# Chunk 0's early work of a fused scan and gated layer in another order

## The chip, the cores and the metric

The kernel runs on one core of one Trainium2 chip. The metric is the device time of one execution in microseconds (us). The core has a matrix engine (TensorE, PE in the profile; its weight loads are PEld), a vector engine (VectorE, DVE), a scalar engine (ScalarE, ACT), a general engine (GpSimd, POOL) and an engine that only issues transfers (SyncE, SP). Each engine works through its own queue in order and waits for the others with semaphores. Transfers between the main memory and the core (DMA) are issued on the queue of SP or ACT.

## The reference

Two parts, the second fed by the first. The first part is a scan over a sequence in chunks, for 4 batches, 8 heads, 768 positions, head size 32 and state size 16:

```python
L = exp(cum[:, :, :, None] - cum[:, :, None, :]) * causal      # decay from j to i
CB = einsum('bhin,bhjn->bhij', Cc, Bc)
y_intra = einsum('bhij,bhjd->bhid', CB * L, xc)
y_inter = einsum('bhin,bhnd->bhid', Cc, state) * exp(cum)[:, :, :, None]
y = y_intra + y_inter
state = decay_full * state + einsum('bhjn,bhjd->bhnd', Bc * decay_from_j, xc)
```

The second part takes y as 3072 rows of 256 numbers: h = x @ w_in (256 x 2048), g = h * cos(h), and out = g @ w_out (2048 x 256).

## The kernel before

The 768 positions are cut into six chunks of 128. Chunks 0 and 1 are cut once more, into four units of 64 positions (0 and 1 are chunk 0), so that the first rows of the second part can start early; the two halves of the partitions (index s) hold two pairs of batches. The order on every engine is written out by hand: instructions stand on an engine's queue in the order of the Python calls, and the framework only adds the semaphores.

Once y of a unit is there, `first` multiplies it by w_in, `wind` and `gate` take the cosine on ACT and DVE, `gated` multiplies, and `second` multiplies by w_out. From about 35 us on these steps alternate on PE without a pause until the end, with the later chunks' scan work in between. The weights come as pieces of 512 KB ("in" 0 to 7, "out" 0 to 7), and `grade` and `join` (L252 to L289) turn each into fp32 on ACT, POOL and DVE.

Units 0 and 1, the part that is changed, go like this:

- The transfers (L291 to L306). ACT's queue issues four loads of C. SP's queue issues a (L213), two halves of B for unit 0 (L294), the first piece of w_in, two halves of x for unit 0 (L297), the first half of B for unit 1 (L298), the second piece of w_in, two halves of x for unit 1, the first piece of w_out, and so on. The second half of B for unit 1 is issued on ACT's queue (L314), after ACT has loaded its table and taken one sine.
- The decays. `share_a` (L346) multiplies the clipped a by a mask of heads: DVE for heads 0 to 5 in one instruction, POOL for heads 6 and 7. `spread_a` (L383) is a matmul that copies these rows to all partitions, into a PSUM bank; the bank's tag ("h", "o" or the pair of "scan") says which buffers it shares. `decays0` (L391) is a scan on DVE from that bank into `lam`. With n=2 each covers half of the heads, 256 columns.
- The turns. Four quarters of C are brought into the order of `c0`, two by POOL (L365) and two by ACT (L366). `turn_c` (L414) transposes them on PE into one bank `tp`. `take_c` (L424) copies unit k's part of this bank twice, each scaled by a mask (column t of `slot`), into `cuts[k]`; both copies run on ACT. `turn_b` (L429) transposes B into another bank on PE, and its return value copies it to `turned` on ACT.
- The product. `inner` (L472) multiplies turned B and `cuts` on PE into the banks g; `weights` (L483) multiplies g by `lam` on DVE; `finish0` (L491) forms y on PE: L504 with the state, L513 for the new state, L521 for the unit itself. `weigh0` (L402) prepares the operand `sc` of L513 on POOL.
- `fill` (L81) are two matmuls on the matrix of ones (L78), ahead of everything else on PE; their results aren't used.

The order of the calls for unit 0 stands in L887 to L915, that for unit 1 in L916 to L923 and in `first_steps` (L1011).

Of the kernel before, what the change touches and what calls it, by code (L numbers as in the profile page):

```python
# [8 lines left out]
FP32 = mybir.dt.float32  # L9
# [3 lines left out]
ALU = mybir.AluOpType  # L13
# [12 lines left out]
def kernel(  # L26
# [12 lines left out]
    nc = tc.nc  # L39
    V, ACT, G, PE = nc.vector, nc.scalar, nc.gpsimd, nc.tensor  # L40
# [3 lines left out]
    P = 128  # L44
# [5 lines left out]
    HH = H // 2  # L50
# [18 lines left out]
    def bank(shape, name, tag):  # L69
        return psum.tile(shape, FP32, tag=tag, bufs=2, name=name)  # L70
# [7 lines left out]
    ones = const.tile([P, P], FP32, name="ones")  # L78
    V.memset(ones, 1.0)

    def fill(dst, times=1):  # L81

        for _ in range(times):
            PE.matmul(dst, lhsT=ones, rhs=ones.unsqueeze(1).to_broadcast([P, dst.shape[1], P]),
                      start=True, stop=True, skip_group_check=True)


    a_all = dram.tile([NB, H, S], FP32, name="a_all")
# [30 lines left out]
    c4 = both[0][:, 1].rearrange("p (h r) n -> p h r n", h=H)  # L119
    xrs = {}  # L120

    def load_b(k, s, eng=nc.sync, of=B):

        eng.dma_start(out=(bs if of is B else cs)[k][s * W:(s + 1) * W].rearrange(
                          "p q (h n) -> p (q h) n", h=H),
                      in_=of[2 * s:2 * s + 2, :, k * W:(k + 1) * W, :]
                      .rearrange("b h i n -> i (b h) n"))
# [7 lines left out]
    def load_x(k, s, eng=nc.sync):  # L135
        if k not in xrs:
            t = loads.tile([P, 2, 2, H, D], FP32, tag="xr", name="xr")
            xrs.update({k // 2 * 2 + i: t[:, i] for i in range(2)})
        eng.dma_start(out=xrs[k][s * W:(s + 1) * W].rearrange("p q h d -> p (q h) d"),
                      in_=x[2 * s:2 * s + 2, :, k * W:(k + 1) * W, :]  # L140
                      .rearrange("b h i d -> i (b h) d"))
# [55 lines left out]
    def load_along(c, seqs=range(NB)):  # L197
# [5 lines left out]
        for b in seqs:  # L203
            for q in range(4 if b % 2 else 1):
# [9 lines left out]
                      in_=a[:, :, 0:P].rearrange("b h (k i) -> (b h) k i", k=2))  # L214
# [15 lines left out]
    def kept(which, i):  # L230
        return (w_in[:, :, i * WC:(i + 1) * WC] if which == "in" else
                w_out[:, i * WF:(i + 1) * WF])

    def fetch(which, i, eng=nc.sync):
        src = (moe_w_in[:, i * WC:(i + 1) * WC].rearrange("(k p) f -> p k f", p=P)
               if which == "in" else
               moe_w_out[i * WF * P:(i + 1) * WF * P, :].rearrange("(f p) m -> p f m", p=P))
        if src.dtype == FP32:
            eng.dma_start(out=kept(which, i), in_=src)
            return  # L240
        words[which, i] = t = conv.tile([P, 2 * WC, 2], U32, tag="words", bufs=8, name="words")
        eng.dma_start(
            out=t.rearrange("p (k f) w -> p k (f w)", k=src.shape[1]), in_=src.bitcast(U32))
# [30 lines left out]
    def join(which, i):  # L274


        parts = held.pop((which, i), ())
        for e, (high, bits, last) in enumerate(parts):
            V.tensor_scalar(out=bits, in0=bits, scalar1=3, scalar2=0x3FFFFFFF,  # L279
                            op0=ALU.logical_shift_left, op1=ALU.bitwise_and)  # L280
            V.scalar_tensor_tensor(out=bits, in0=high, scalar=0xC0000000, in1=bits,  # L281
                                   op0=ALU.bitwise_and, op1=ALU.bitwise_or)
            dst = kept(which, i)
            if len(parts) > 1:
                dst = dst[:, :, e * P:(e + 1) * P]
            else:
                bits, last = (ap.rearrange("p (k f) -> p k f", k=dst.shape[1])
                              for ap in (bits, last))
            G.tensor_tensor(out=dst.bitcast(U32), in0=bits, in1=last, op=ALU.add)  # L289
# [5 lines left out]
    fetch("in", 0)  # L295
    for s in range(2):
        load_x(0, s)  # L297
    load_b(1, 0)  # L298
    fetch("in", 1)
    for s in range(2):  # L300
        load_x(1, s)
# [2 lines left out]
        out=a_in, in_=a.rearrange("(u b) h (c p) -> (b h c) u p", u=NU, p=P))  # L304
# [6 lines left out]
    quarter = const.tile([P, 1], FP32, name="quarter")  # L311
    V.memset(quarter, HALF_PI)
    ACT.activation(const.tile([P, 1], FP32, name="sine"), quarter, AF.Sin)
    load_b(1, 1, nc.scalar)  # L314
    V.memset(a0z[:, :, 0:1], 0.0)
    for r in (slice(NB * H, W), slice(W, P)):
        V.memset(a0z[r, :, 1:], 0.0)
# [28 lines left out]
    def share_a(k, eng, h0, h1):  # L346
        eng.tensor_tensor(out=a0s[k][:, h0:h1],
                          in0=a0z[:, k:k + 1].to_broadcast([P, h1 - h0, W]),
                          in1=mine[:, h0:h1].unsqueeze(2).to_broadcast([P, h1 - h0, W]),
                          op=ALU.mult)  # L350

    share_a(0, G, 6, H)
    share_a(0, V, 0, 6)
    whose_of(1)
    G.memset(along1[:, :, 0:1], 0.0)
    G.tensor_scalar(out=a0[:, 1], in0=a0[:, 1], **clip)
    for p in range(2):
# [4 lines left out]
                  in_=mine.unsqueeze(2).to_broadcast([P, H, N]))  # L362
    c0 = loads.tile([P, 2, 2, 4, 2, N], FP32, tag="blocks", name="c0").rearrange(
        "p a b c d n -> p (a b c d n)").rearrange("p (r h n) -> p r h n", r=4, h=H)
    G.tensor_copy(out=c0[:, 0:2].rearrange("p r h n -> p h r n"), in_=c4[:, :, 0:2])  # L365
    ACT.copy(out=c0[:, 2:4].rearrange("p r h n -> p h r n"), in_=c4[:, :, 2:4])  # L366
    G.memset(lead, 0.0)
    G.memset(lead[:, :, 0:1], 1.0)
    slot = const.tile([P, 2], FP32, name="slot")
# [10 lines left out]
    lams, scs, turns0, cuts, gs, m_of, rTs, states0 = {}, {}, {}, {}, {}, {}, {}, {}  # L380
    spread = {}

    def spread_a(k, p, i=0, n=1, tag="o"):  # L383

        ps = (pair("a_ps")[:, 0] if tag is None else bank([P, 4 * P], "a_ps", tag))
        ps = spread[k, p, i] = ps[:, 0:H * W // n].rearrange("p (h i) -> p h i", i=W)
        PE.matmul(ps, lhsT=whose[:, p].rearrange("p s i -> p (s i)"),
                  rhs=a0s[k][:, i * H // n:(i + 1) * H // n], start=True, stop=True,
                  skip_group_check=True)

    def decays0(k, p, i=0, n=1):  # L391

        if p == i == 0:
            lams[k] = scan.tile([P, 2, H, W], FP32, tag="lam", bufs=4, name="lam")
        flat = "p h i -> p (h i)"
        hs = slice(i * H // n, (i + 1) * H // n)
        rows_ = spread.pop((k, p, i)) if k < 2 else arows[k][:, p]
        V.tensor_tensor_scan(out=lams[k][:, p, hs].rearrange(flat), data0=rows_.rearrange(flat),
                             data1=unit0[:, hs].rearrange(flat), initial=0.0,
                             op0=ALU.mult, op1=ALU.add)  # L400
# [13 lines left out]
    def turn_c():  # L414

        tp = bank([P, 4, P], "tp", "o")
        for r in range(4):
            PE.transpose(tp[:, r], c0[:, r].rearrange("p h n -> p (h n)"), ident)
        tp = tp.rearrange("p r (b k g) -> p k b g r", b=NB, k=2)

        def of(k, dst, **v):
            ACT.activation(dst.rearrange("p b (g r) -> p b g r", r=4), tp[:, k], AF.Copy, **v)

        def take(k):  # L424
            for t in range(2):
                of(k, cuts[k][:, t].rearrange("p q (s i) -> p (q s) i", s=2), scale=slot[:, t:t + 1])
        return take, of

    def turn_b(k, tp):  # L429

        for p in range(2):
            PE.transpose(tp[:, 2 * k + p], bs[k][:, p], ident)
        return lambda: ACT.copy(out=bTs[k], in_=tp[:, 2 * k:2 * k + 2])
# [38 lines left out]
    def inner(k, t):  # L472

        gs[k, t] = g = pair("g")
        bT, cT = bTs[k], cuts[k]
        for p, s, q in ((p, s, q) for p in range(2) for s in range(2) for q in range(2)):
            ss, q_ = slice(s * W, (s + 1) * W), 2 * t + q
            r = slice(32 * q_, 32 * q_ + 32)
            PE.matmul(g[ss, q, p * P:(p + 1) * P].rearrange("p (t i) -> p t i", t=2),  # L479
                      lhsT=bT[r, p, ss], rhs=cT[r, :, p, ss], start=True, stop=True,  # L480
                      tile_position=(32 * q_, s * W), skip_group_check=True)
# [221 lines left out]
    hp, turns, gT, o = {}, {}, {}, {}  # L703
# [180 lines left out]
                              in_=ob[s * W:(s + 1) * W].rearrange("p h m -> p (h m)"))  # L884


    fill(bank([P, 4, P], "warm", "o"), 1)  # L887
    fill(bank([P, 2, P], "warm", "o"), 1)
    spread_a(0, 0, 0, 2, None)
    spread_a(0, 0, 1, 2, None)  # L890
    spread_a(0, 1, 0, 2, "h")
    for p, i in ((0, 0), (0, 1), (1, 0)):
        decays0(0, p, i, 2)
    spread_a(0, 1, 1, 2, "h")
    decays0(0, 1, 1, 2)
    spread_a(1, 0, 0, 2, None)
    decays0(1, 0, 0, 2)
    take_c, of_c = turn_c()
    tp_b = bank([P, 4, P], "tp", "o")
    take_b = turn_b(0, tp_b)  # L900
    spread_a(1, 0, 1, 2, "h")
    decays0(1, 0, 1, 2)
    take_c(0)
    take_b()
    weigh0(0)
    grade("in", 0)
    for t in range(2):
        inner(0, t)
    spread_a(1, 1, tag="h")
    for q in range(2):  # L910
        weights(0, q)
    take_c(1)
    join("in", 0)
    decays0(1, 1)
    take_s0, _ = finish0(0)  # L915
    take_b = turn_b(1, tp_b)  # L916
# [262 lines left out]
```

## Time and profile before

| | |
|---|---|
| time, median of 3 runs | 369.6 us (369.3 to 369.76) |
| the profiled execution's own time | 369.82 us |
| its span in the profile | 368.0 us |
| PE busy | 361.3 us (98%) |
| DVE busy | 276.2 us (75%) |
| ACT busy | 173.0 us (47%) |
| POOL busy | 217.6 us (59%) |

The span is measured between the first and the last instruction of the program; 1.8 us of the execution's own time lie around it. Busy shares are means over the whole span; the stretch that the change touches is its first 18 us, and there they are different. In the first 36 us, by the table of busy time in each stretch, PE is busy for 33.3 us, DVE for 30.1, ACT for 23.0 and POOL for 22.9, and from about 3 to 28 us the 16 DMA engines are busy nearly without a gap.

In the lines of the timeline, the two first numbers are the start of a group of instructions and its time, then come the engine, the source line, the operation, the tile written and the tiles read, and in brackets how long the engine was idle before and what ended that. A queue of an engine (SPq, ACTq) issues transfers. In the chain, the number after a tile is the source line.

### The profile page before, as it was taken

The page shows a single profiled execution, that of the slowest core. Times are in us where ns is not written, and L with a number is a line of the kernel's source. Part 1 is how long each engine was busy: PE and PEld are TensorE (multiplying, and loading weights), DVE is VectorE, ACT ScalarE, POOL GpSimd, SP SyncE. Part 2 cuts the span into 40 slices and gives each one's busy share as a digit, 9 for nine tenths or more (in the row PEclk, how much of TensorE's full clock was granted, in tenths as well). Part 3 has the DMA queues.
Part 4 walks back from the last instruction along what each step waited for, and adds up shares of the span by engine and source line. Part 5 has one row for each costly group of instructions (what it writes and reads, how often), then busy time and mean ns, then how long its engine had stood idle before and what let it go on. Part 6 is the DMA issues. An engine that isn't in the chain of part 4 may idle for free.

```text
span 368.0 us, 8760 instructions
## 1 busy us (share of the span) xinstructions
PE 361.3 (98%) x3390; PEld 325.4 (88%) x3390; DVE 276.2 (75%) x451; ACT 173.0 (47%) x300; POOL 217.6 (59%) x340
## 2 busy tenths in 40 slices
PE   8999999999999999999999999999999999999995
PEld 5688888889999899999999999899999989999995
DVE  7789998578699858978867987777887783544463
ACT  3597757454445345354344444434444534444442
POOL 6567747579786558765446674544584444554441
PEclk9999999999999999999999999999999999999999
DMA  9995948457226746731055341020100010010011
GB/s 139 239 373 141 186 112 134 56 146 190 73 77 89 137 111 90 215 94 32 6 78 115 93 130 45 0 53 2 24 18 2 0 30 2 2 29 2 0 30 30
DMA packets 97706, 30.57 MB, mean 83 GB/s; under 512 B 71456, under 2 KB 93568, under 8 KB 97664
## 3 DMA queue, kind: packets, MB, share of 16 engines
q1 hardware_dynamic: 95376, 29.55, 35.4%
q10 hardware_dynamic: 2288, 0.46, 0.8%
q8 instruction: 27, 0.44, 0.5%
q14 instruction: 15, 0.12, 0.1%
HBM read 26.58 MB, written 3.34 MB: 81 GB/s over the span
## 4 chain that ended last, share of the span: by engine, by line
PE 91%; DVE 3%; DMA 2%; ACT 2%; issue 1%; SPq 1%; ACTq 0%
PE hp L724 44%; PE o L833 34%; PE o L795 6%; DMA xr<-in_x_dram 2%; PE y L674 2%; PE g L622 2%; DVE mag L279 1%; PE y L654 1%; PE y L521 1%; DVE mag L281 1%; PE g L479 1%; PE y L504 1%; DVE w L737 1%; PE o L878 1%; ACT mag L266 0%
## 5 line engine op out<-in xcount | busy, mean ns | idle before, releaser
L724 PE MATMUL hp<-yT,w_in 128*128 128x256 f32 x768 | 183.2, 382 | 0.3 <-DVE gT L751 0.3
L724 PEld LDWEIGHTS hp<-yT,w_in 128*128 128x128 f32 x768 | 139.3, 190 | 19.9 <-issue 3.2
L776 POOL TENSOR_TENSOR gd<-gT 128x256 f32<-128x256 f32 x79 | 60.0, 760 | 96.7 <-DVE gT L751 84.6
L746 ACT ACTIVATE w<-w,quarter 128x512 f32<-128x512 f32 x96 | 69.2, 721 | 84.4 <-DVE w L737 84.3
L737 DVE SCALAR_TENSOR_TENSOR w<-hp,k 128x512 f32<-128x512 f32 x96 | 65.8, 686 | 43.2 <-ACT k L731 43.0
L731 ACT ACTIVATE k<-hp 128x512 int32<-128x512 f32 x96 | 57.1, 594 | 78.9 <-PE hp L724 78.5
L751 DVE TENSOR_TENSOR gT<-hp,w 128x512 f32<-128x512 f32 x96 | 65.3, 680 | 33.2 <-ACT w L746 21.7
L833 PE MATMUL o<-words,gd 128*128 128x128 f32 x474 | 65.9, 275 | 0.0
L833 PEld LDWEIGHTS o<-words,gd 128*128 128x128 f32 x474 | 59.3, 192 | 0.0
L833 PEld LDWEIGHTS o<-w_out,gT 128*128 128x128 f32 x316 | 47.5, 191 | 4.0
L779 POOL TENSOR_TENSOR gd<-gT,gd 128x128 f32<-128x128 f32 x79 | 46.0, 582 | 6.2
L833 PE MATMUL o<-w_out,gT 128*128 128x128 f32 x316 | 48.0, 274 | 0.0
L778 POOL TENSOR_TENSOR gd<-gT,gd 128x128 f32<-128x128 f32 x79 | 44.0, 556 | 6.2
L581 DVE TENSOR_TENSOR_SCAN lam<-arow,unit 128x512 f32<-128x512 f32 x32 | 42.0, 1314 | 0.0
L833 PE MATMUL o<-words,gT 128*128 128x128 f32 x158 | 30.6, 275 | 0.0
L833 PE MATMUL o<-w_out,gd 128*128 128x128 f32 x158 | 30.5, 275 | 0.0
L795 PE MATMUL o<-w_out,gT 128*128 128x256 f32 x128 | 29.9, 379 | 0.0
L795 PEld LDWEIGHTS o<-w_out,gT 128*128 128x128 f32 x128 | 24.2, 190 | 3.3
L643 DVE TENSOR_TENSOR m<-g,lam 128x256 f32<-128x256 f32 x64 | 24.7, 414 | 0.4
L833 PEld LDWEIGHTS o<-w_out,gd 128*128 128x128 f32 x158 | 24.0, 192 | 0.0
L833 PEld LDWEIGHTS o<-words,gT 128*128 128x128 f32 x158 | 24.0, 192 | 0.0
L850 DVE TENSOR_TENSOR sum<-ps,sum 128x256 f32<-128x256 f32 (+1 forms) x27 | 16.6, 640 | 0.6
(113 smaller groups left out, 282.1 us busy)
## 6 DMA issues: line engine op xcount, KB each, us to landing
arow<-a_cut SPq DMA_DIRECT2D x16, 512.0 KB
words<-in_moe_w_in_dram SPq DMA_DIRECT2D x8, 512.0 KB
words<-in_moe_w_out_dram SPq DMA_DIRECT2D x8, 512.0 KB
out_dram<-sum SPq DMA_DIRECT2D x18, 128.0 KB
xr<-in_x_dram SPq DMA_DIRECT2D x16, 128.0 KB
xr<-in_x_dram SPq DMA_DIRECT2D x16, 64.0 KB
bc<-in_B_dram SPq DMA_DIRECT2D x15, 64.0 KB
arow<-a_cut SPq DMA_DIRECT2D x2, 256.0 KB
```

Source lines behind the costliest of these rows:

```text
L581: V.tensor_tensor_scan(out=lam[c, b][:, hs].rearrange("p h i -> p (h i)"), data0=rows_.rearrange("p h i -> p (h i)"), data1=unit[:, b % 2 ...
L643: V.tensor_tensor(out=m_[js, :, :, is_], in0=g_[js, :, :, is_], in1=l_[js, :, :, is_], op=ALU.mult)
L724: PE.matmul(to_[:, e], lhsT=w_in[:, k, fs], rhs=y[:, k], start=(k == 0), stop=(k == KT - 1), skip_group_check=True)
L731: ACT.activation(k, hp[n], AF.Copy, bias=0.25, scale=INV_2PI)
L737: V.scalar_tensor_tensor(out=w, in0=hp[n], scalar=INV_2PI, in1=k, op0=ALU.mult, op1=ALU.subtract)
L746: ACT.activation(cos, cos, AF.Sin, bias=quarter, scale=TWO_PI)
L751: V.tensor_tensor(out=gT[n], in0=hp.pop(n), in1=cos, op=ALU.mult)
L776: G.tensor_tensor(out=d[:, 0:2], in0=g[:, 1:2].to_broadcast([P, 2, P]), in1=g[:, 3::-3], op=ALU.subtract)
L778: G.tensor_tensor(out=d[:, 2], in0=g[:, 0], in1=d[:, 0], op=ALU.subtract)
L779: G.tensor_tensor(out=d[:, 3], in0=g[:, 2], in1=d[:, 2], op=ALU.subtract)
L795: PE.matmul(o[c, u][:, t], lhsT=g[:, 2 * e + t], rhs=w_out[:, 2 * j + e], start=(j == e == t == 0), stop=(j == NJ - 1 and e == 1), skip_gr ...
L833: PE.matmul(at[q], lhsT=a_[q], rhs=w[q], start=(j == 0 and q in starts), stop=(j == NJ - 1), skip_group_check=True)
```

## The change

The change has five parts. The fills take their operands from a constant column that the program's preamble writes, instead of the matrix of ones that DVE writes. Unit 1's second half of B is issued on SP's queue behind its first half, and so behind unit 0's x and ahead of the second piece of w_in, and no more on ACT's queue. DVE's share_a for unit 0 is cut into heads 0 to 3 and heads 4 and 5. C's quarters go to POOL (three) and ACT (one), and ACT's is placed behind the copy of turned B. In the calls, B of unit 0 is turned ahead of the fourth and fifth spread_a and ahead of C; the second of the two copies of C for unit 0 runs on DVE; the sixth spread_a stands behind `inner`, and its scan behind `join`.

```diff
-    def fill(dst, times=1):
-
-        for _ in range(times):
-            PE.matmul(dst, lhsT=ones, rhs=ones.unsqueeze(1).to_broadcast([P, dst.shape[1], P]),
-                      start=True, stop=True, skip_group_check=True)
+    def fill(dst):
+
+        n = dst.shape[1]
+        PE.matmul(dst.rearrange("p q i -> p (q i)"),
+                  lhsT=nc.const_aps.tensor(1.0, (P, P), FP32),
+                  rhs=nc.const_aps.tensor(1.0, (P, n * P), FP32),
+                  start=True, stop=True, skip_group_check=True)
...
-    load_b(1, 0)
+    for s in range(2):
+        load_b(1, s)
     fetch("in", 1)
...
-    load_b(1, 1, nc.scalar)
...
-    share_a(0, V, 0, 6)
+    share_a(0, V, 0, HH)
+    share_a(0, V, HH, 6)
...
-    G.tensor_copy(out=c0[:, 0:2].rearrange("p r h n -> p h r n"), in_=c4[:, :, 0:2])
-    ACT.copy(out=c0[:, 2:4].rearrange("p r h n -> p h r n"), in_=c4[:, :, 2:4])
+    G.tensor_copy(out=c0[:, 0:3].rearrange("p r h n -> p h r n"), in_=c4[:, :, 0:3])
...
             for t in range(2):
-                of(k, cuts[k][:, t].rearrange("p q (s i) -> p (q s) i", s=2), scale=slot[:, t:t + 1])
+                dst = cuts[k][:, t].rearrange("p q (s i) -> p (q s) i", s=2)
+                if k == 0 and t == 1:
+                    V.tensor_scalar(out=dst.rearrange("p b (g r) -> p b g r", r=4), in0=tp[:, k],
+                                    scalar1=slot[:, t:t + 1], scalar2=None, op0=ALU.mult)
+                else:
+                    of(k, dst, scale=slot[:, t:t + 1])
...
     for p, i in ((0, 0), (0, 1), (1, 0)):
         decays0(0, p, i, 2)
+    tp_b = bank([P, 4, P], "tp", "o")
+    turn_b(0, tp_b)()
+    ACT.copy(out=c0[:, 3:4].rearrange("p r h n -> p h r n"), in_=c4[:, :, 3:4])
     spread_a(0, 1, 1, 2, "h")
     decays0(0, 1, 1, 2)
-    spread_a(1, 0, 0, 2, None)
+    spread_a(1, 0, 0, 2, "h")
+    take_c, of_c = turn_c()
+    take_c(0)
     decays0(1, 0, 0, 2)
-    take_c, of_c = turn_c()
-    tp_b = bank([P, 4, P], "tp", "o")
-    take_b = turn_b(0, tp_b)
-    spread_a(1, 0, 1, 2, "h")
-    decays0(1, 0, 1, 2)
-    take_c(0)
-    take_b()
     weigh0(0)
     grade("in", 0)
     for t in range(2):
         inner(0, t)
+    spread_a(1, 0, 1, 2, "h")
     spread_a(1, 1, tag="h")
     for q in range(2):
         weights(0, q)
     take_c(1)
     join("in", 0)
+    decays0(1, 0, 1, 2)
     decays0(1, 1)
```

More of the change, by code (lines that the diff above doesn't have):

```diff
@@ L884, in last_step @@
                               in_=ob[s * W:(s + 1) * W].rearrange("p h m -> p (h m)"))
-    fill(bank([P, 4, P], "warm", "o"), 1)
-    fill(bank([P, 2, P], "warm", "o"), 1)
+    fill(bank([P, 4, P], "warm", "o"))
+    fill(bank([P, 2, P], "warm", "o"))
     spread_a(0, 0, 0, 2, None)
```

## The prediction

> **What bounds the kernel now.** I read the page's chain of work that ended last, then the same chain in order of time for the first 36 us, then the timelines of single engines there, and at last the transfers in short windows.
>
> ```profile
> PE 91%; DVE 3%; DMA 2%; ACT 2%; issue 1%; SPq 1%; ACTq 0%
> 4.21 7.18 DMA xr<-in_x_dram
> 11.44 0.37 PE y L513 x20
> 12.58 0.58 ACT yT L532
> 13.16 0.28 ACT turned L433
> 13.49 1.19 PE g L479 x32
> 14.69 1.06 PE hp L724 x4
> 15.74 0.85 PE y L504 x31
> 17.60 0.65 ACT yT L530 x2
> ```
>
> From 34.7 us on the chain is TensorE almost alone (the 91%), in steps that the change doesn't touch. What happens before moves the end one for one: from 17.6 to 34.7 the chain goes through ACT and DVE queues in order, with no transfer on it. So I ask one thing: when does unit 1's y end, 17.58 us in this execution (ACT takes it at 17.60)? The chain blames x's second half, landed at 11.39. But a chain shows the last wait, and others end close behind it:
>
> ```profile
> 6.47 0.41 ACT L366 COPY c<-bc 128x256 f32<-128x256 f32 x1 [1.69 <-DMA bc<-in_C_dram]
> 7.65 0.84 ACT L422 ACTIVATE cT<-tp,slot 128x256 f32<-128x256 f32 x2 [0.77 <-PE tp L418]
> 8.38 0.37 ACT L433 COPY turned<-tp 128x256 f32<-128x256 f32 x1
> 7.50 1.49 DVE L398 TENSOR_TENSOR_SCAN lam<-a_ps,unit 128x256 f32<-128x256 f32 x2
> 9.54 0.69 DVE L488 TENSOR_TENSOR m<-g,lam 128x512 f32<-128x512 f32 x1 [0.54 <-PE g L479]
> 11.80 1.22 DVE L398 TENSOR_TENSOR_SCAN lam<-a_ps,unit 128x512 f32<-128x512 f32 x1
> 13.39 0.70 DVE L440 TENSOR_TENSOR_SCAN m<-a_ps,m 128x260 f32<-128x260 f32 x1 [0.37 <-PE a_ps L438]
> 14.23 1.29 DVE L488 TENSOR_TENSOR m<-g,lam 128x512 f32<-128x512 f32 x2
> 14.32 0.68 POOL L448 TENSOR_TENSOR rT<-c,m 128x256 f32<-128x256 f32 x1 [1.01 <-ACT c L422]
> 15.55 0.64 POOL L404 TENSOR_TENSOR sc<-bc,lam 128x256 f32<-128x256 f32 x1
> ```
>
> DVE is almost full: between its multiplication for unit 0 (L488, 9.54) and that for unit 1 (14.23) it idles 0.37 + 0.14 us. The latter frees the banks that y of unit 1 writes; its second instruction ends at 15.52, y's matmuls (L504) start at 15.67, and L513 waits for POOL's sc, done at 16.19. DVE is as late here as x.
>
> Beside its instructions the trace records when each transfer's 16 increments arrive. Of the last ones I need: unit 0's second half of B 6.68, C 6.45, x's second half 11.39, unit 1's first half of B 11.92, the second piece of w_in 14.05, unit 1's second x 16.06. One of the sixteen is always late: B's other fifteen were there by 5.50.
>
> **What the Trainium skill says.** PSUM — Partial Sum Buffer, section "PSUM bank collisions raise a hardware error": two engines may not access one bank in the same quadrant at once, two readers included, so the accesses are put in order. In the stretch I read of the trace of before no bank has two readers at once, so it neither supports nor contradicts this. DMA: Bandwidth & Descriptors, "Issuing engines are not separate DMA queues": transfers from several engines run on the same DMA engines and interleave. The trace agrees: from 7 to 8 us ACT's queue moved 818 packets and SP's 533, 1351 together, and SP's alone 1329 from 12 to 13 us. TensorE: Matmul & The Clock Gate, "What's actually happening": the array runs at half rate until a busy window of about 3.4 us has passed, and falls back after an idle one. Here 256-column passes start 0.427 us apart until 5.06 and 0.216 from 5.78 on, and an idle stretch of 0.5 us from 8.27 left it fast. VectorE: DVE Perf Modes, "Why PSUM operands drop a tier": fp32 from PSUM goes at one element a cycle; the nearest row is 0.41 us (L643, 128x256 from PSUM).
>
> **The change, part by part.**
>
> *Fills.* They wait for nothing now and start near 0.73 instead of 1.06: four passes, done 0.33 us earlier (3.45 for 3.78).
>
> *share_a in two pieces.* 0.56 us for 384 columns becomes two pieces; the first (about 0.4) releases the first spread_a at 3.37, the two together cost DVE about 0.07 more. With the fills the first scan starts near 4.65 instead of 4.96. Both are worth 0.3 us only if nothing later waits.
>
> *B turned ahead of C.* On TensorE's queue the two transposes of B now stand before the fourth and fifth spread_a, and they wait for B's second half, 6.68. In before they stood behind C's and waited for nothing. The third spread_a is done at 5.85, so TensorE stands still until 6.73. Then: 2 transposes x 0.109 = 6.95; two spread_a, four passes x 0.216 = 7.81; four transposes of C x 0.109, the last started at 8.14, with its latency 8.41 (before: 7.61). What hides behind this: scan four on DVE, 7.59 instead of 6.92; turned on ACT, 7.15 to 7.53, no longer on the path; C's copies, POOL's with three quarters (0.40 for two, 0.29 for one, so about 0.51, done 7.01) and ACT's quarter by 7.7. So the 0.3 us from fills and share_a are lost, and C's transposes are 0.80 late.
>
> *cT on two engines.* Both halves read one bank, tp, of 128 x 512 fp32. In the built program DVE's half waits for ACT's half, and TensorE's g waits for DVE's: they run in series. ACT 0.47 (8.45 to 8.92), a handover of 0.04, DVE 0.41 (to 9.37), so g starts at 9.41. In before it was 1.19 us from C's transposes to g (two halves and turned, overlapping, 7.61 to 8.80); now 1.00. That gives 0.19 back. Net: g at 9.41 instead of 8.80, +0.61. DVE's queue has the fifth scan behind its half: 9.3 to 9.97, done before g's end (9.41 + 0.74 = 10.15).
>
> *scan of (1,0,1) and its spread_a moved behind g.* TensorE: 0.43 us in front of y, which waits for the multiplication on DVE anyway. DVE: multiplication of unit 0 from 10.15 to 11.44; the join's two instructions to 12.50; now a scan of 0.67 (12.41 to 13.08), formerly before 9.54; scan of 1.22 (to 14.21); scan of reach 0.70 (14.13 to 14.83); multiplication for unit 1 at 14.75. Before: 14.23. As a sum: +0.61 for the late start, +0.59 for a scan (start to start in a row of them), -0.51 for the idle time that disappears, -0.16 because two instructions then start 0.08 before the end of the one ahead, as those in a row do: +0.53.
>
> *x's transfers ahead.* B's second half of unit 1 leaves ACT's queue (issued 3.52, packets from 6.66 to 8.92, in between x's) and stands behind x on SP's. Lower bound of the gain: nothing; upper: 1.24 us, its engine time. I take 0.8, x at 10.6. It isn't worth anything: y of unit 0 needs its second multiplication, 11.44, and TensorE's spreads end at about 11.3; y ends at 12.5, as before (12.56). Unit 1's B lands near 12.0 on the same total of packets; its transposes are due then. Moved past on SP: w_in's second piece and all behind it. As one queue alone moves as much as two did, I leave their landings as they are; the other bound is 1.24 later (second rival).
>
> *The end.* Multiplication for unit 1 ends at 16.04, L504 starts at 16.10 (+0.43), takes 0.85; POOL's rT, mag and sc follow the scan of reach: sc done at 16.7, in time for 16.95; L513 0.2, L521 0.86: y ends at 18.0. **+0.4 us.** It passes through ACT's full queue (2.00 of 2 us busy from 18 to 20, from 22 to 26 too) to the end. The profiled execution took 369.82 (span 368.0 and 1.8 around it), so 370.2; on the median of 369.6, which is 0.2 below it, **370.0 us**.
>
> **The rivals.**
> 1. *B is there in time.* Were B's last increment at 5.7, as the other fifteen are, TensorE wouldn't stand still; C's arrival (6.45) and POOL's copy set the transposes at 7.07 to 7.67, g starts at 8.69, the first multiplication at 9.43, the one for unit 1 about 0.2 earlier: 369.4. For it: fifteen of sixteen; against it: the late one is late in every transfer I looked at. If, beyond that, the halves of cT did overlap, another 0.4 at g, of which unit 1's g (13.15) lets through 0.15: 369.2.
> 2. *Slower: the words wait behind B.* If the two queues did overlap their costs, w_in's second piece lands up to 1.24 late, 15.3 instead of 14.05. ACT's mag for it, POOL's mag and then sc queue behind it in order. It decides from a landing of 14.7 on (POOL is free for mag at 15.5, ACT's takes 0.7). At 15.3: sc done at 17.3, y ends at 18.45, **370.5**. Unit 1's second x (16.06 + 1.24 = 17.3) says the same. The following words have 0.5 us of slack (the first of w_out lands 17.62, used 18.13), so more may be lost there: up to 371. For it: 1.9 queue-shares busy in 7 to 8 us when both are at work; against it: the equal packet counts above.
> 3. *The array goes slow.* It now idles 0.9 us from 5.83 and about 1 us before g. If this counts as an idle window, the four passes of spread_a cost 0.21 more each, and with something for the six transposes g is about 1.0 later: +1.4, 371.0. Against it: the gaps of 0.5 and 0.6 us in before did nothing, and the window named above is longer.
> 4. *Pairing of DVE and POOL in 24 to 34 us.* DVE's L279 takes 0.42 alone and 1.41 at 26.04, beside POOL's L289. A shift that isn't even can add or remove one such delay, 0.7 either way: 369.3 or 370.7.
>
> **How the numbers follow.** Forecast, +0.2 to +0.7: 0.48. Rival 1: 0.17. Rival 2: 0.13. Rival 3: 0.07. Rival 4: 0.15, two thirds of it slower. 0.2%, 0.74 us, is about what a measurement of this kernel can tell from no change, so faster is under 368.9 and slower over 370.3. No single case is faster by that much; the good sides of rivals 1 and 4 together, and what I don't see, get 0.08. Slower: most of rivals 2 and 3, the slow side of 4 and what is left of the forecast's upper end, 0.34. No change: 0.58. The range goes from 369.3 (rival 1) to 371.0 (rivals 2 and 3).
>
> **What would show it.** In the profile after: TensorE's transposes of B (two, before two spread_a) waiting for a DMA of B until about 6.7; DVE's half of cT starting only at the end of ACT's; g at 9.4; DVE without a gap from 10.1 to 16; the multiplication for unit 1 at 14.7; y of unit 1 ending at 18.0; x no longer on the chain. I'm wrong if B lands by 6, if w_in's second piece lands after 14.7, or if a 256-column pass after 6 us takes 0.427.

## The result and the profile after

The changed kernel takes 370.38 us in the median of 22 runs (369.82 to 371.58), the kernel before 369.43 in the median of 22 runs beside them (369.13 to 370.34). The ratio is 1.0023, with a 95% interval of 1.0016 to 1.0030: 0.85 us slower (0.6 to 1.1). The forecast was 370.0, a loss of 0.4. The loss is clear of zero; as a share, 0.23% with 0.16 to 0.30, it lies on both sides of the 0.2% that the prediction took for the least that a measurement of this kernel tells. The profiled execution took 370.09 us, with a span of 368.3.

The page's shares of the chain that ended last, changed kernel:

```profile
PE 92%; DVE 3%; ACT 2%; issue 1%; POOL 0%; ACTq 0%
```

The transfer of x, 2% of the chain before, is gone from it. What is there in its place is in the same chain in order of time (start, length, what; the number after a tile is the source line):

```profile
5.52 1.28 DVE lam L400 x2
6.85 0.70 PE a_ps L389 x2
7.54 0.45 PE tp L420 x4
8.02 0.48 ACT cT L424
8.53 0.49 DVE cT L430
9.07 0.73 PE g L486 x32
9.79 1.49 PE a_ps L389 x4
...
15.86 0.61 POOL sc L406
16.52 0.46 PE y L520 x32
16.98 0.59 PE y L528 x32
17.59 0.65 ACT yT L537 x2
```

The two halves of cT stand one behind the other, ACT's and then DVE's, and g follows DVE's. Unit 1's y ends at 17.59. The timeline of DVE and of POOL's sc (in brackets the idle time ahead of a group and what ended it):

```profile
8.53 0.48 DVE L430 TENSOR_SCALAR cT<-tp,slot 128x256 f32<-128x256 f32 x1 [1.13 <-ACT cT L424]
8.93 0.68 DVE L400 TENSOR_TENSOR_SCAN lam<-a_ps,unit 128x256 f32<-128x256 f32 x1
9.80 1.29 DVE L495 TENSOR_TENSOR m<-g,lam 128x512 f32<-128x512 f32 x2 [0.19 <-PE g L486]
12.07 1.80 DVE L400 TENSOR_TENSOR_SCAN lam<-a_ps,unit 128x256 f32<-128x256 f32 x2
13.78 0.67 DVE L447 TENSOR_TENSOR_SCAN m<-a_ps,m 128x260 f32<-128x260 f32 x1
14.37 1.26 DVE L495 TENSOR_TENSOR m<-g,lam 128x512 f32<-128x512 f32 x2
15.83 0.64 POOL L406 TENSOR_TENSOR sc<-bc,lam 128x256 f32<-128x256 f32 x1
```

From 9.80 on DVE doesn't stop until unit 1's multiplication (14.37) is done. The group of 1.80 us at 12.07 holds the moved scan, (1,0,1), and the larger one that was there before (1.22 alone).

Three things in this execution are not as forecast. B's last increment arrived at 5.69 us, not 6.68, so TensorE didn't stand still for it until 6.7. What it waits for ahead of C is a scan: the fifth spread_a starts at 6.85, when DVE's third scan is done (6.79). The diff gives this spread_a the tag "h" and with it the buffer that the third had; neither the list of the change's parts nor the prediction names that wait, which B's at 6.7 would have covered. And unit 1's y ends at the same time as in the first profile of before (17.60), where x was late. So this pair of profiles doesn't show where 0.85 us are lost.

### The profile page after: what moved, and what is told of

Read it like the earlier page. It is cut to its first block, busy times and chain, and to the rows that moved or that the text cites. A ratio compares the mean times of both kernels' runs of the same rounds, so it can differ in the third digit from the quotient of the medians.

```text
span 368.3 us, 8763 instructions
## 1 busy us (share of the span) xinstructions
PE 361.6 (98%) x3390; PEld 325.4 (88%) x3390; DVE 276.7 (75%) x453; ACT 172.5 (47%) x299; POOL 215.7 (59%) x340
## 4 chain that ended last, share of the span: by engine, by line
PE 92%; DVE 3%; ACT 2%; issue 1%; POOL 0%; ACTq 0%
PE hp L731 43%; PE o L840 33%; PE o L802 6%; PE y L681 2%; PE g L629 2%; PE a_ps L389 1%; DVE mag L281 1%; PE y L528 1%; PE y L661 1%; PE warm L84 1%; DVE mag L283 1%; ACT mag L268 1%; DVE w L744 1%; PE g L486 1%; PE o L885 1%
## 5 line engine op out<-in xcount | busy, mean ns | idle before, releaser
L785 POOL TENSOR_TENSOR gd<-gT,gd 128x128 f32<-128x128 f32 x79 | 44.0, 557 | 6.2
L786 POOL TENSOR_TENSOR gd<-gT,gd 128x128 f32<-128x128 f32 x79 | 43.8, 554 | 6.2
```

The lines of the kernel that those rows point to most:

```text
L785: G.tensor_tensor(out=d[:, 2], in0=g[:, 0], in1=d[:, 0], op=ALU.subtract)
L786: G.tensor_tensor(out=d[:, 3], in0=g[:, 2], in1=d[:, 2], op=ALU.subtract)
```

## The experiments

Two theories stood at first. A: DVE is the bound; the loss is DVE's half of cT in series and the scan behind the join. B: TensorE waits for B, which stands ahead of C, and everything behind it is late. Each result below gives the median and, in us, what the ratio to the kernel before says with its 95% interval (369.4 us times the ratio less one); the changed kernel stands at +0.85 (0.6 to 1.1) on this scale. The runs below form four groups (four, four, three and one), each measured beside the kernel before, which took 369.37, 369.31, 369.5 and 369.33 there.

**Both kernels once more, unchanged.**

> The kernel before, unchanged, for a second profile. Theory A (DVE is the bound of the changed kernel; the kernel before waits for x's late increment in its first profile) expects that x's second half lands earlier here than the 11.39 us of the first profile in an execution near the median of 369.4, that the multiplication for unit 1 then starts near 13.9 instead of 14.23, and y of unit 1 ends near 17.2 instead of 17.58. Theory B (B's late increment holds TensorE in the changed kernel) says nothing of this run but expects B's last increment to lie anywhere between 5.6 and 6.7.

> The changed kernel, unchanged, for a second profile. Theory B: in an execution at or above the median of 370.4, B's last increment lands later than the 5.69 us of the first profile, up to 6.7, and g starts later than 9.07, up to 9.4; the time follows it. Theory A: even with B in time the multiplication for unit 1 starts at 14.3 to 14.4, with DVE without a gap from the product of unit 0 on.

One execution each: 369.71 and 369.66 us. A single execution doesn't separate the kernels. Their traces show what varies by itself: B's last increment at 5.86 and 5.83, so the 6.68 of the first profile was the exception (of fourteen traces it is the only one above 6.1). The matrix engine's clock was granted in full from 6.45 in one and 4.27 in the other (5.64 and 5.51 before), and g starts at 9.05 and 8.76. TensorE's passes of 256 columns start 0.43 us apart ahead of that moment and 0.22 behind it, so the start of g follows a moment that the kernel doesn't set alone. And in this execution of before x is no longer last:

```profile
9.79 1.29 DVE L488 TENSOR_TENSOR m<-g,lam 128x512 f32<-128x512 f32 x2 [0.54 <-PE g L479]
10.99 0.41 DVE L279 TENSOR_SCALAR mag<-mag 128x512 uint32<-128x512 uint32 x1
11.44 0.69 DVE L281 SCALAR_TENSOR_TENSOR mag<-words,mag 128x512 uint32<-128x512 uint32 x1
12.05 1.22 DVE L398 TENSOR_TENSOR_SCAN lam<-a_ps,unit 128x512 f32<-128x512 f32 x1
13.18 0.67 DVE L440 TENSOR_TENSOR_SCAN m<-a_ps,m 128x260 f32<-128x260 f32 x1
13.77 1.26 DVE L488 TENSOR_TENSOR m<-g,lam 128x512 f32<-128x512 f32 x2
```

That is the same row as in the changed kernel, without the moved scan. From g to the multiplication for unit 1 it takes 13.77 - 9.05 = 4.72 us; in the changed kernel 14.37 - 9.07 = 5.30.

**Both halves of cT on ACT again**, in the changed kernel:

```diff
-                if k == 0 and t == 1:
-                    V.tensor_scalar(out=dst.rearrange("p b (g r) -> p b g r", r=4), in0=tp[:, k],
-                                    scalar1=slot[:, t:t + 1], scalar2=None, op0=ALU.mult)
-                else:
-                    of(k, dst, scale=slot[:, t:t + 1])
+                of(k, dst, scale=slot[:, t:t + 1])
```

> The changed kernel with both halves of cT on ACT. If the two halves run in series anyway (0.48 on ACT, 0.03 handover, 0.48 on DVE, from C's transposes to g 1.05), ACT alone takes 0.84 for both, g starts 0.15 earlier, DVE gets 0.4 of free time: 0.1 to 0.3 us faster than the changed kernel, 370.1 to 370.3. If the halves did help by running side by side, this is slower than the changed kernel by 0.3 us.

369.84 us, +0.41 (0.18 to 0.66): about half of the loss is gone. From C's first transpose to g it now takes 1.53 us (7.51 to 9.04) instead of 1.69 (7.38 to 9.07). That is only 0.16, so the series alone doesn't account for 0.4.

**The scans of unit 1's first half in DVE's idle time ahead of g**, in the changed kernel (both parts back to the front of the product):

```diff
+    decays0(1, 0, 0, 2)
     take_c, of_c = turn_c()
+    spread_a(1, 0, 1, 2, "h")
     take_c(0)
-    decays0(1, 0, 0, 2)
+    decays0(1, 0, 1, 2)
...
-    spread_a(1, 0, 1, 2, "h")
...
-    decays0(1, 0, 1, 2)
```

> The changed kernel with the scans of unit 1's first half put into DVE's idle stretches: one ahead of DVE's half of cT, one behind it and ahead of unit 0's multiplication, with the sixth spread_a ahead of g on TensorE. Theory A: DVE's queue from 9.8 us on loses 0.6, TensorE's 0.43 between g and y; the multiplication for unit 1 starts near 13.8 instead of 14.37; 0.4 to 0.6 us faster than the changed kernel, 369.8 to 370.0. Theory B: B's wait stays, so no more than 0.2 faster.

369.53 us, +0.30 (0.07 to 0.55). From g to unit 1's multiplication it is 4.72 us again (8.73 to 13.45), 0.58 less.

**Both of these together.**

> The changed kernel with both halves of cT on ACT again and the scans of unit 1's first half in DVE's idle time ahead of g. Theory A (the loss is DVE's: a half of cT in series, and a scan behind the join): the whole loss is gone, 0.7 to 1.0 us below the changed kernel and at or below the kernel before, 369.0 to 369.5, with unit 1's multiplication at 13.2 to 13.7. Theory B (TensorE that stands still for B and runs its passes slow is the loss): it stays 0.3 us or more above the kernel before, 369.7 to 370.3. From the two single edits as they measured (0.5 and 0.85 below the changed kernel) a sum would be 369.0.

369.28 us, -0.11 (-0.41 to 0.22): the whole loss is gone, and nothing beyond it is won. DVE in the profile of this run:

```profile
7.06 1.27 DVE L400 TENSOR_TENSOR_SCAN lam<-a_ps,unit 128x256 f32<-128x256 f32 x2 [0.60 <-PE a_ps L389]
8.54 0.69 DVE L400 TENSOR_TENSOR_SCAN lam<-a_ps,unit 128x256 f32<-128x256 f32 x1 [0.21 <-PE a_ps L389]
9.55 1.29 DVE L491 TENSOR_TENSOR m<-g,lam 128x512 f32<-128x512 f32 x2 [0.32 <-PE g L482]
...
11.82 1.22 DVE L400 TENSOR_TENSOR_SCAN lam<-a_ps,unit 128x512 f32<-128x512 f32 x1
...
13.54 1.26 DVE L491 TENSOR_TENSOR m<-g,lam 128x512 f32<-128x512 f32 x2
```

All scans of 256 columns are done ahead of 9.55, in time that DVE had to spare. B is still turned ahead of C here, the fills, share_a and x's transfers are those of the changed kernel, and TensorE stands 0.99 us in front of B's transposes. So together these cost nothing that the runs can tell, though a small loss of one that a gain of another covers isn't excluded. That is against theory B.

**B turned behind C again**, in the changed kernel (the transposes and the copy behind `take_c(0)`).

```diff
-    turn_b(0, tp_b)()
...
     take_c, of_c = turn_c()
+    take_b = turn_b(0, tp_b)
     take_c(0)
+    take_b()
```

> The changed kernel with B's transposes and their copy behind C's first half again. Theory B (TensorE waits for B): 0.3 us or more below the changed kernel, 369.5 to 370.0. Theory A: B is there by 5.9 us in nearly every execution, so the transposes of B cost nothing ahead of C that they don't cost behind it; 370.1 to 370.6, within 0.2 us of the changed kernel.

370.29 us (7 runs), +1.03 (0.63 to 1.44): no better than the changed kernel. But the edit doesn't free TensorE. With B's transposes gone from in front, the fifth spread_a waits for the third scan all the longer:

```profile
6.67 0.70 PE L389 MATMUL a_ps<-m 128*128 128x256 f32 x2 [0.50 <-DVE lam L400]
```

So this run doesn't price the wait for B by itself. Theory B falls by the run with both edits, which has that wait and no loss. The fifth spread_a's own wait (its first pass starts 0.40 to 0.88 us behind the pass ahead in five of the seven traces of the changed kernel and its variants without small matmuls, 0.22 in the other two) was given back by no run, so what it costs is open.

**Single parts of the change, made in the kernel before.** x's transfers ahead of unit 1's second half of B:

```diff
-    load_b(1, 0)
+    for s in range(2):
+        load_b(1, s)
...
-    load_b(1, 1, nc.scalar)
```

> The kernel before with one part of the change: unit 1's second half of B issued on SP behind x instead of on ACT's queue. Theory A (DVE is the bound, x is hidden behind DVE's load): x's second half lands near 9.8 instead of 10.8 to 11.4, y of unit 0 starts at most 0.5 us earlier, the multiplication for unit 1 still starts at 13.7 to 14.2, and the time falls by 0 to 0.2 us (369.2 to 369.4 against 369.4). Rival (x carries the kernel before): the whole 1 us arrives, 368.4 to 368.9. If B of unit 1 or w_in were late now, the time would rise by 0.3 or more.

369.38 us, -0.07 (-0.37 to 0.22). x lands at 9.85 instead of 10.84, and it is worth nothing, as theory A has it. Fills from the constant column (with the changed kernel's `fill`) and share_a in two:

```diff
-    share_a(0, V, 0, 6)
+    share_a(0, V, 0, HH)
+    share_a(0, V, HH, 6)
...
-    fill(bank([P, 4, P], "warm", "o"), 1)
-    fill(bank([P, 2, P], "warm", "o"), 1)
+    fill(bank([P, 4, P], "warm", "o"))
+    fill(bank([P, 2, P], "warm", "o"))
```

> The kernel before with two parts of the change: the fills read a constant column and share_a for DVE is cut in two. The first scan starts 0.2 to 0.3 us earlier. Theory A: DVE is full from the first scans to unit 1's multiplication except for the wait for C and cT, which the transfer of C sets, so that at most 0.1 to 0.2 us arrives: 369.2 to 369.4. If the early scans are on the path, 0.3 us: 369.1.

369.34 us, +0.04 (-0.26 to 0.33): nothing either. And the scan (1,0,1) behind g and the join (the expectation counts it as the fifth; it is the sixth):

```diff
-    spread_a(1, 0, 1, 2, "h")
-    decays0(1, 0, 1, 2)
...
         inner(0, t)
+    spread_a(1, 0, 1, 2, "h")
...
     join("in", 0)
+    decays0(1, 0, 1, 2)
```

> The kernel before with one part of the change alone: the fifth spread_a and scan, (1,0,1), behind g and behind the join. Theory A (this scan is the loss): from g to unit 1's multiplication 5.30 us as in the changed kernel instead of 4.72, and the time rises by 0.5 to 0.9 us (369.9 to 370.2 against 369.3). If the half of cT on DVE carries a share of its own, as its removal from the changed kernel suggests (0.4 us less), this stays nearer to 0.3: 369.6.

369.64 us, -0.04 (-0.33 to 0.30). (The two medians are 0.14 us apart the other way; one run of 371.26 among the 17 of the kernel before moves the ratio.) In the profile the scan does what theory A says: 5.30 us from g (9.02) to the multiplication (14.32). But the time doesn't rise by 0.5. This was a miss of theory A, and the question is what else holds unit 1's y in the kernel before. TensorE in p_before2's profile has a standstill in the middle of that y, to which the profile gives no releaser ("issue"), and the kernel with the moved scan has none:

```profile
15.12 0.68 PE L504 MATMUL y<-rT,state 32*64 32x64 f32 x28
16.10 0.33 PE L504 MATMUL y<-rT,state 32*64 32x64 f32 x4 [0.30 <-issue]
```

```profile
15.47 0.98 PE L504 MATMUL y<-rT,state 32*64 32x64 f32 x32
16.48 0.46 PE L513 MATMUL y<-xr,sc 64*32 64x64 f32 x32
```

So in these two executions the earlier multiplication runs into a standstill, and unit 1's y ends at 17.43 in p_before2 and at 17.55 with the scan moved: of 0.55 us 0.12 are left.

**Where the standstill comes from.** In five of the twelve traces of kernels without small matmuls TensorE stands before its 221st matmul (the expectation below calls it the 220th), for 0.12 to 0.64 us. On the queue that the page names "instruction", one packet of 16,384 bytes lands shortly before: at 14.83 in p_before2, and TensorE goes on at 16.10; at 15.51 with both halves of cT on ACT, and it goes on at 16.79. In no trace does it pass this matmul less than 1.27 us after the landing. The test puts 14 small matmuls (32 x 32, on the constant column, in a loop `small`) in place of the last 384 columns of the fills, in the kernel before and in the kernel with both edits, and so moves the work against the places in TensorE's stream:

```diff
-    fill(bank([P, 4, P], "warm", "o"), 1)
-    fill(bank([P, 2, P], "warm", "o"), 1)
+    fill(bank([P, 3, P], "warm", "o"), 1)
+    small(bank([P, 2, P], "warm", "o"), 14)
```

> The kernel before with 14 small matmuls (32 x 32) in place of the last 384 columns of the fills, which moves every later instruction of TensorE 56 places on in its stream and nothing in the work. Theory F (four of the profiles show TensorE standing 0.1 to 0.6 us with no releaser in y of unit 1, always before its 220th matmul, some 1.3 us behind the landing of a 16 KB instruction transfer: it waits for instructions): the standstill moves 28 matmuls forward, to the start of that y, where TensorE waits for DVE anyway, the transfer starts earlier, and the time falls by 0.2 to 0.4 us (369.0). If the standstill is one of profiled executions alone, or has another cause: no change, 369.2 to 369.4, and in the second case still before the matmul that was the 220th.

> The changed kernel with both halves of cT on ACT, the scans in DVE's idle time, and the 14 small matmuls. Theory F: y of unit 1 runs through, and the multiplication, which is 0.1 to 0.2 us earlier here than in the kernel before, counts: 368.8 to 369.0, below both kernels. Otherwise as without the small matmuls, 369.2 to 369.4.

375.46 us (4 runs), +5.7 (4.9 to 6.5), and 375.79 us (5 runs), +6.2 (5.3 to 7.2). Neither theory expected anything like it. TensorE (in this run's lines L513 is y from the state and L733 is hp) and, in the second fence, the table of windows (busy time by engine, then the granted clock, the share of the DMA engines and GB/s), both of the first of the two runs:

```profile
14.79 0.32 PE L513 MATMUL y<-rT,state 32*64 32x64 f32 x2
15.83 0.69 PE L513 MATMUL y<-rT,state 32*64 32x64 f32 x30 [0.72 <-issue]
...
17.55 0.70 PE L733 MATMUL hp<-yT,w_in 128*128 128x256 f32 x2
22.13 6.21 PE L733 MATMUL hp<-yT,w_in 128*128 128x256 f32 x20 [3.88 <-issue]
```

```profile
18.00:22.00 4.00, 0.25 (x2) 0.00 (x0) 0.00 (x0) 0.73 (x2) 0.61 (x1) 1.00 1.04 383
22.00:25.50 3.50, 3.37 (x8) 2.73 (x9) 1.45 (x3) 1.67 (x4) 0.00 (x0) 0.51 0.85 315
25.50:28.00 2.50, 2.50 (x13) 2.19 (x13) 1.42 (x3) 1.64 (x3) 1.27 (x1) 1.00 0.37 126
```

The 14 calls are 28 matmuls of the trace, 26 more than those they replace (with the weight loads 52 instructions, not the 56 of the expectation). The first standstill has moved by just these 26: it comes behind 2 matmuls of that y instead of 28, before the 221st matmul of the stream as ever. A second one of 3.88 us stands before the 349th, 128 matmuls later; the other kernel has one of 4.37 us before the 348th (some matmuls can be missing from a trace). So the standstill belongs to the place in the stream, not to the work. The next instruction packet lands at 20.88, and TensorE goes on 1.25 us later, near the 1.27 to 1.51 us seen at the first. In all kernels without the small matmuls the 349th is due only at 23.0 to 24.3, after the packet, and nothing is seen there.

The Trainium skill has instructions refilled in blocks of 16 KiB, 256 of them, by a DMA queue of the engine's own, and the cost of crossing the border of a block mostly hidden (Runtime: NRT & Kernel Launch, "Instruction fetch mechanics"). The size agrees with the packet, and 128 matmuls with 128 weight loads make 256. But the cost is not hidden here. The packets don't come earlier for a TensorE that is 26 matmuls further (they start at 12.8 and 19.8, in the other traces at 12.7 to 13.3 and 19.5 to 21.2), so that crossing early cost 0.1 to 4.4 us.

In all fourteen traces the second packet starts 3.7 to 5.1 us after the 221st matmul. The 128 matmuls from there are 100 short ones of y and 28 long ones of hp in the kernel before, which take 7.5 us; with the 26 at the front they are 126 and 2, and TensorE is through at 18.25, 2.4 us after it went on at 15.83. That fits a packet that is asked for only when TensorE crosses the border before. This wasn't tested, nor was it that the full DMA engines (share 1.04) are what delays the packet. Behind the pause the granted clock is at half, from 22.04 to 25.45 us: 8 matmuls in 3.5 us where p_before2 does 18 in the same window, by estimate another 1.7 us (half of 3.4).

**One instruction more on ACT.** What half of cT on DVE costs beyond its 0.16 us shows in part late in the traces. In all four traces with that half on DVE, and in none of the nine others without this copy, three of ACT's instructions k<-hp (143, 272 and 279 us) start about 0.3 us late, and 0.11 to 0.14 us are lost for good between the 33rd and the 41st gT (138 to 165 us; the expectation counts them from 0). ACT has one copy fewer there. The test gives it one back, which does nothing needed:

```diff
     take_c(0)
+    ACT.copy(out=const.tile([P, 1], FP32, name="spare"), in_=slot[:, 1:2])
```

> The changed kernel with one instruction more on ACT, a copy of 128 x 1 right behind its half of cT, where ACT is idle; nothing else is different. Theory S (taking a half of cT from ACT costs little where it stands, but it moves every later instruction of ACT one place ahead in its stream, and then three of ACT's readings of hp, near 143, 272 and 279 us, start 0.3 to 0.45 us late with nothing to wait for, as in all four traces with that half on DVE and in none of the seven others): the three late starts are gone, the 0.12 us lost from the 32nd to the 40th gT is gone, and the time falls by 0.1 to 0.5 us, to 369.9 to 370.2. Rival (the half on DVE costs its time in the series ahead of g): no late loss goes away or it doesn't count, 370.2 to 370.5.

370.19 us (18 runs), +0.74 (0.48 to 1.00). ACT in the changed kernel, and then with the copy:

```profile
142.36 0.59 ACT L850 COPY ps<-o 128x512 f32<-128x512 f32 x1
143.59 0.60 ACT L738 ACTIVATE k<-hp 128x512 int32<-128x512 f32 x1 [0.64 <-PE hp L731]
```

```profile
142.31 0.59 ACT L850 COPY ps<-o 128x512 f32<-128x512 f32 x1
143.26 0.60 ACT L738 ACTIVATE k<-hp 128x512 int32<-128x512 f32 x1 [0.36 <-PE hp L731]
```

The late start is gone with the copy, 0.36 us of idle time instead of 0.64, and so are the two others and the loss (no time is lost from the 33rd to the 41st gT against the kernel with both edits). The profile names hp as the releaser, but hp wasn't later. So the late start goes with the place in ACT's stream, by one instruction, and not with hp; what makes that place late is open. The median is 0.1 to 0.2 us under the changed kernel's, which is what the trace gives, but within the intervals. By the medians the larger share of what cT's move to DVE costs isn't this.

No version is faster than the kernel before: the one with both edits equals it.

## Why the prediction was right in sign and small in size

*The bound.* Right. DVE is full from the first multiplication to the last, and x isn't the bound: 1 us earlier in the kernel before it changed nothing.

*Fills and share_a.* Right that nothing arrives (+0.04 on their own), but not only because TensorE then waits for B: nothing arrives in the kernel before either, where it doesn't. There TensorE works from the first spread_a to C's transposes with no gap that the profile shows, and the new fills start it earlier (3.48 instead of 3.78; 4.85 instead of 5.06 from the fourth pass on). But its passes are slow until the clock is granted in full, and that moment didn't come earlier in this run's profile (6.31; 5.64 and 6.45 in the kernel before's two). C's first transpose starts at 7.08, against 6.96 and 7.26. Passes that start 0.43 us apart, and then 0.22, make of 0.2 us at the slow pace 0.1 by estimate, less than the runs can tell.

*B turned ahead of C.* This step failed. It took 6.68, the arrival of one late increment in one execution, for a property of the transfer. In the other traces B is complete by 5.3 to 6.1. C's transposes were forecast 0.80 late; the first of them starts at 7.08, 7.32 and 7.38 in the changed kernel's traces and that with the copy on ACT, and at 6.96 and 7.26 in before's two: 0.15 late. The next step gives 0.1 us back, and g starts at 8.76 to 9.07 against 8.80 and 9.05, where +0.61 was forecast. That g isn't late at all isn't shown by this, since the full clock came earlier in the changed kernel's three (4.27 to 5.51 against 5.64 and 6.45); in the pair with the nearest grants, 5.51 and 5.64, g is 0.27 late. What holds TensorE ahead of C differs: in the first profile the third scan (6.85), which the step put at nothing, in the second B's arrival at 5.83 (0.58 us idle). Turning B behind C again brought nothing, as TensorE then waits for that scan.

*cT on two engines.* Right: the halves run in series (8.02 to 8.49, 8.53 to 9.01, g at 9.07). DVE's half takes 0.48 us, where 0.41 was taken from another instruction, so the step gives back 0.1 and not 0.19. The Trainium skill's rule that two engines may not read one bank of PSUM at once, so that a dependency is put between them (PSUM — Partial Sum Buffer, "PSUM bank collisions raise a hardware error"), now has a case that agrees with it, though a dependency put in for another reason would look the same. What the step left out is that ACT's later instructions move one place in their stream, 0.12 us.

*The scan behind the join.* Right to the hundredth: +0.59 forecast from a row of scans, 5.30 - 4.72 = 0.58 measured. But its value depends on the end. In the changed kernel, putting the scans back takes away 0.55; in the kernel before, moving the scan costs nothing that can be told, and in the profile the standstill for instructions covers it.

*The end.* That the delay passes through to the end is right for the first stretch: from unit 1's yT to the fifth gT it takes 16.29 to 16.34 us in the twelve traces without small matmuls. Beyond, the step is short by at least 0.2: the 0.12 on ACT, and 0.09 behind the last gT (6.70 and 6.72 us to the end, 6.62 and 6.60 before). All nine traces with the change's transfers of x have 6.68 to 6.89 there and the five others 6.58 to 6.62, so it comes with these; why is open.

*The rivals.* B was in time, as the first had it, but the kernel didn't come to 369.4, since that figure counts on the same idle time of DVE as the sum below. Words behind B: the second piece of w_in lands at 12.93, not 15.3; the 1.9 queue-shares that spoke for it are 1.74 in the table of transfers from 7 to 8 us (100.5% and 73.1%). The array going slow and the pairing of DVE and POOL: neither is in the changed kernel's traces; the join's first instruction (L281 there, L279 before) takes 1.40 us beside POOL at 26.06, as 1.41 at 26.04 before.

*So the sum.* +0.61 at g was wrong, or far too large, and +0.59 for the scan right; the idle time that was to take 0.51 of them back, and 0.16 with it, isn't there in before's usual execution, where DVE has no such gap (4.72 us from g instead of the first profile's 5.43). Two errors nearly cancelled, and that is luck: 0.53 at the multiplication became 0.58 between g and it. It starts at 14.06 to 14.37, not 14.75, and y ends at 17.32 to 17.59, not 18.0, since g isn't at 9.41.

*What stays open.* The multiplication's 0.58 us and the two late losses of 0.2 give some 0.8 if all arrives, about what was measured. But in the profiled executions it doesn't all arrive (370.09 and 369.66 against 369.82 and 369.71), and the scan alone in before cost -0.04 (-0.33 to 0.30). All five executions with the standstill lie above their kernel's median, by 0.11 to 0.59 us, and of the seven without it one does (the first of before, where x was late); before's usual executions may have less of it than its profiled ones. That would explain both, and wasn't shown. Nor is it shown where the rest of the 0.4 us lies that cT's half on DVE costs.

## What to carry to other kernels

Look at a second execution before an arrival in the profile is made the base of a step: one late increment, or the time at which the clock is granted, moves an early stage by as much as a small change does. On an engine that is full, count what is moved in front of the result that others wait for: a scan in idle time is free, behind the join it cost its whole length at the next multiplication (0.58 us), unless another wait covers it. A new bank for a tile is a new wait too: count whose reading has to end first. And an instruction added to or taken from TensorE shifts all later work against the borders of its instruction stream; in a stretch with full DMA engines such a border cost from 0.1 to 4.4 us here, so a change of a few instructions has to be measured with the count held equal before its effect is put down to the work.

## What was not expected of the hardware

TensorE stood up to 4.4 us for an instruction packet of 16 KB in a stretch in which the DMA engines were full, each time until 1.25 to 1.5 us after the packet had landed, at places 128 matmuls apart. 14 matmuls of 32 x 32 in place of 384 columns of the fills made a kernel of 369.5 us one of 375.5. After the pause the clock was at half for 3.4 us. The clock's first full grant came between 3.9 and 6.5 us in fourteen traces.
